# The same instructions of a fused forward and backward kernel in another order, with other PSUM banks

## The chip, the cores and the metric

The kernel runs on one core of a Trainium2 chip. The metric is the device time of one execution in microseconds (us). Before the change three runs took 435.45, 432.09 and 433.91 us, median 433.91. A core has the engines PE (matmul), DVE (vector), ACT (scalar), POOL and SP; each runs its own list of instructions strictly in order, and they meet through semaphores. In this kernel SP only issues DMAs.

## The reference

The output is `x + A(LN(x)) + B(LN(x))` and its gradients with respect to all inputs that take part, for one sequence of 2048 tokens with 512 channels, in bf16. A is a long convolution with a state space kernel, done by FFT, and B a bilinear gated MLP with 1376 hidden features:

```python
def A(q, k, v, shift_k, ssm_k, ssm_D):
    k_shift = causal_shift_conv(k, shift_k)          # 4 taps
    kv = k_shift * v
    y = irfft(rfft(pad(kv)) * rfft(pad(ssm_k)))[:S]  # per channel, L = 2 S
    return q * (y + kv * ssm_D)

def B(x, w_gate, w_up, w_down):
    return ((x @ w_gate) * (x @ w_up)) @ w_down

xn = layernorm(A_q)
out = A_q + A(xn, A_k, A_v, A_shift_k, A_ssm_k, A_ssm_D) + B(xn, B_w_gate, B_w_up, B_w_down)
# returned: out and the vjp of grad_out for the nine inputs
```

(`causal_shift_conv`, `pad` and `rfft` abbreviate the reference's own lines.)

## The kernel before

The Fourier transforms are matrix products in three steps (a first, a middle and a last DFT) with two transpositions through DRAM between them: the first writes to a DRAM tile `AX`, the middle one reads it and writes `CX`, the last one reads `CX`. The MLP runs in six strips of features; its hidden values and their gradients go to a DRAM tile `HD`.

The stages overlap, but their bulk comes in this order. The MLP strips (`mlp_rows`, `hd_store`) run beside the first DFT (`a_gen`). The weight gradients (`dw_gen`) run beside the middle DFT: `s_load(i)` reads from `AX`, `s_B` multiplies, `s_pw` is the pointwise product on DVE, `s_Bi` multiplies back, ACT copies the result out of PSUM, and four stores per step write it to `CX`. The last stage, called the F stage here, has eight steps n = 0 to 7 of two row blocks each:

- `c_load(n)` (L650) reads 1.5 MB of `CX` into one buffer `f["C"]`; for n = 0 it is split into four quarters of 384 KB, one for each quarter of `CX`'s tokens; the last quarter waits for the last four stores to `CX`, those of `s_Bi(7)`
- `last_dft(n)` (L694) does 12 matmuls on that buffer, within `c_dkv(n)` (L712); `c_load(n + 1)` can overwrite the buffer only when they are done
- `hd_load(n)` (L616) is one transposing DMA from `HD` into one of two buffers; `y_o` and `y_x` (L759, L776) multiply from it with the weights `wy`, in groups of 11 and 22 matmuls
- `c_dkv`, `c_dsk`, `dk_pair` and `c_o5` are DVE and ACT work on the convolution's gradients, with small loads and the output stores. In `c_dkv(n)` for n < 2 three small copies move rows across partitions (L712 on).

All of the 274 DMAs go through SP's one queue. SP issues them in its order; each waits for its own dependences, and also for the DMA eight places ahead of it to have landed, since eight semaphores serve the DMAs in turn. So one DMA that waits, or whose issue takes long, holds all behind it.

The order is neither that of the source nor that of a scheduler at build time. The function body records each operation as an `Op` with its engine (the call is made at L173, so every instruction in the profile carries that line). Groups of matmuls into one PSUM tile make one operation. The last line, `emit(PLAN)`, decodes a string constant at L33: 2321 numbers of two bytes, the order in which the operations are issued, and one byte for each of 408 PSUM tiles, its bank:

```python
order = struct.unpack(f"<{len(ops)}H", raw[:2 * len(ops)])
for s, b in zip(slots, raw[2 * len(ops):], strict=True):
    s.base = Q[b // 2] if s.n == 2 else halves[b]
...
    for i in order:
        for fn in ops[i].fns:
            fn()
```

Each engine's list is the part of this order that is its own: 1019 operations on PE (3174 matmuls), 654 on DVE, 371 on ACT, 274 on SP and 3 on POOL. Who waits for whom follows from the tiles and buffers that they share, in the order issued.

Of the kernel before, what the change touches and what calls it, by code (L numbers as in the profile page):

```python
# [17 lines left out]
S = 2048  # L18
D = 512
F = 1376  # L20
R = 16
# [3 lines left out]
SF = [0, 1280, 256, 512, 768, 1024]  # L25
# [4 lines left out]
RING = 28  # L30
RO = [0, 16, 24, 40, 56, 72]
EPS = 1e-5
PLAN = "c-lP|1FSC1uI&_au5H`4ZQHhO+qP}nwr$%s-*@hxyv)wFskUu4MPxt#hyu|e21J5%kRCEa2FM7RAPZ!LT#ya2LvF|ec_AM-U=UC+@DKzcAS8r>&=3Z~LO2Ky?H~f=fTR!;qC!Nd1;rp5#D=&K3(7+rC<^f)KBR>N;3Wklgk+E(DnLOf06C!$)P{;s2?|4TC;_FQG8BO-Pz|a=V`u{1p(*r$p3n?>!Dy%s?V&W(ff`T~2Ekw`3B92nG>7`o0s25c=nG?@E_8(c&;rInD;Nj!pe4+Q6>tPPL2GCL3!pO$fPpX`y1+u101e?WOocWu5hg(y=n7?F8nlI@Fdb&XZWscyU=eJD#jq5Xz$VxXTi_E+hD$IEX22d83M*j>#KjA+4A#IZh==iUD-4HiFdKHjcGw9Ca4jr{UGN!3z<$^ZA0ZK>hQyEx(!d<}1tVcK9DsfB1-`;TSO<q-J)D4(a14&aDL4(^AS5QlM3@-UVG=wC=`krL!{m4kZox&k4CmoG+<+_a9j?M{xCuYtCxpV3kOY#$ANT+j@gdxY6qpiI;RARAk03Rs!L;}cLSq<=h)*FbhQsg}0asxL%!rvVGiJf8$XE%pVP&j>*|93-z?_&1b7M8kgL$z!8Y&9r!@F<?&ca{Vh=hQMjj#qb#wOSlo8eGwjxDeyK8IE~3|~NNY=dpFCPv1n7zJx#ZES~iurAia_Baw>!zefm<={80#MQV4*Wx-{k8@!IguqC+AERLq=0}I!U^%L6LXV@cJ`TqYI09cn1MG;e;0?Tkw{QR(;%FR$8?XRQ#7Q_7$Kf;_j}ve@&cK=22@B#ZEQGVMFc!hixEZ(LHtd33u^V>B9@rCm;XGV`i?BBq#Xi^<n^8Y3hW&8>4#Yut5a;4#+>3{B3LeHII3E|{VqAhtaVt*6=va%kV{;meF>nPI#}ZhVVqt8oPbIMh)uuW4ga%SQiit;Y5DlgwG?b3xFgk_}s3p~*M%0joQxj@R?WqHu#8Oxq%V1e7hvo4EPN&m2gU;Y7Y)j{`0=A>ecm=OwREkE?DF(%)Yj_=F(G9$bx9~RJ!Mk`5@8bh}h_UGr#-X_M7@y!%e1`GpIljP`_zGX+8+?oJ@I8LOj~JigV1GJ~7jY(Cz*#h#E>bI+Lp$&je#S5O6~Ezk{DD957yiaS_!ohYh#Vy#CZU9sh!T^Mk*B#dg630ex<r?09$lfUv>S)u0BQt{={=mqeRu{g;Z({_L6n1XQZC9(A*dJa#9i2%_TYIMMR_PBC8Ok&f>Kf_3Qegf427j|l$Y{RcuGxaC@qzs{8W-kQE4heWvLuRpmda;GEjL+LP;qiWuyuei6T=)sze2-AQhs*RD_CBF)B`(s4``yEL4T6QZ>p-*{C`#q#Cq@I#M_4M2n~g^`!1}jTX~&8cAKKGxeqQG@3Th7FtVvXe_O!Z8V0q(l}a2YiK)7pdECOp3*aVPA_N@ZKO@Km-f>{+DVgX8kroTWwehD&>#9iyXhv~pqF%nR?uNuN>k_p-GlK|lUCAl`b)p)H~pkt^or2Ep;L69z`dr2befJ)825l4(Qyjv!nyG71iht`<lF~(M`!3grFH3CdY8dvbeY^OT1AiPBQ2o2beql+yE~NGWpP<uHkaL*%i%uJJ@W1gMRZ^3Gv#z~TrQW}#dYzVxcDxC3+0Bmgf5Xw?4rA2F0_l_hPudZxEtX{I(0!Vgp1;)xu`CN8|_B9Brd6o=3=>+Zn{h6lDiphyvySzx|uGoo8Tt73a+B7<i1fG`c5GvNTN_kS%wiLqC}F)u8OPbX1P!jT4uYku9{2Xs=F`}R>Db2m&#3X<J@EyULwn4m)b><t~B2*bSqpM*N<Ym{H~KL;0n4zuCOcOin?O1xGUj0yJ)h+EpiK7ESc+~N(_l3@g%w=kl3=!#g&*6Uy?{7NhpaWnWU7Gu8XVTYPwpklq>DZxU#OCOD(A+jg)s?T{qX=^>961ZI@QkNqVW{GD;>H<LbJ4u9xfW`nbNXzU$|*O9pA+a!P;K&^2-cTn=gM2D&D$sT<^yN(xCXxnzzjEK6M>$t`)LnQQL0xE5}!Yw4;<E7#hsbk(JX6q8jhi?nfVT{daw+Pl@Rjue$5QbI~fDJd?crHqu73Q}ImNkyqFm86PPm8`PHZFBcr2Ukz(N=LWWt#jL5K6jKdOHC;#1tg#3mHaZ;)t6e*KsHltx$hphhwhPk?4G!%?wNb;UbvU;m1`oe-5dATHI)zUqx<AOyD#pmYbftrGifZ1<eU5Mez?T^(<R~cZi8zsNjVuO=M<chQ*j4rFFRcq=_s9~t8|mj(p`E;FX<`0rJwYdzS2Tk%3w*&Y512*%jq~hXW$_+R7T2gx8G&ty)F}vlF@R&4U>H?GmntnZjU?U`p9s}%70vIX)A4{m4tNdWQ-hi17wg4lx#dl=E_8wB$FjO{|yW=$T@k6<Y3}lJXNO2CU@4IbLZU!w?Q_$i>@eNa+_qMjFZdmiW@Jvd7<oZ#dw0umwB>S^6(;AAWLPrtd=FRQkKaoSs`O3lG{V)0%dTz%#ztMQ)WnUKH*Nf&2rUUbJtx-zTs}VTkf_y=C())-YTVdo9vL|Zo3?DkvK9(;i#OK%kWw`>Q1@!vPMq3b&`)yisRi9jiYl6j>)k&Hpk((e8<IO=F)sh&d6ywFBfE|>~hQ9E}7?q_sCwk>kdjyJ|wlcI_Ky3d{}C50p2H7IRPi+f_zra$wj#&)%c2BmaB424#<8<#D(~=Je4P+Z0tFRLvTobAde&zm*voWS8DSOxh2=7Fc;xET#j$bL%A>aBn*e;id>!#yN&L+9Fe1POkPMOuE4M4r8MQ1+?B&|E3U$Kq#3`K(;S|gb2mQ2-T5rPl{eCY32sYe{x09-r~HsM{7(MJZ}}^~0;6YZMkRIHgL`sA?!~>i5BKE={6XH!8TU+{%L$q4zRG6_rHwcu*XMrRpYL;M4WnVT0YBh}99|!BIK9htc>p(I(I90FsrUE^*JIPi96{UiKpw>J`J;T1zx+wwyT}TXg(GStZOp3eIEs2rq#-n+e&A>tRnKupZqMhr6L;WPfx+l0zvaO^gkx(Qjjltv3wP$k`izt7J5Hi0HJK*W)S6aPXhuz?={1d}(@dIKGiVHrsTcSqU*zYULtpU={>bq(fyURkno~(G@nz1cSNJM_;#@j|XYwq*#@Bf^-{5STTW@l9{i%UsE_wA9&*8Z|kLPnf&7=8s0Wai5yqK5pQZAssbQu@a+gw<e^DrLHD|iHt<e&VSvuJ63!)3Ib7SZxrNy};lt)dmRvR2co`h{y~b*-tjw6@mKx>`>QX)!ITCAGMg(h@p~ckyl>&0}~hkK^$?fhY1F-pl*=J5S>Me1H$~WIn`Gcq$*}BYc#P@o_%EC;1ou;Awn{8|g~^%1v}SgZ<XOfuFFkHq}+Un%D4JZl=xk8-M2C{D<pnUtPy-w5_h^4ZM-tX?yLb{k4HM)Q!4{H}e1;sDreFZsCr)l{@Ku?W|q2t8UWGx<$8YH{GV&b%zetAv#od>Mp&i-L;4I)Lz<KxAAt~!Pj+|4%ZPnQb*}%y{%)kk6zOodRG_dZr!5`b&)RCCAw6X>2h76dv%|#)cv|jS8EGxsjan@#<vhAvXdX^9lfVx^^c;FvE1QtDz-+~>N-83>ouyWg|qM$(Sj_RMX>QYK_}`YJ*1QMp&r&FIz^A_F+Hv)^rTMJX*ykJ=qWv|Gj*2E)|)y<=juE?qi6M;p4SU{Q6t$S4QY`rifzzadQj)<C5>gdETt8;B9_!1Yg$WZMeVhwx0n{n!kAfD^A_9USTT!kX)Kkcws>|~^H>s#YghD%zR_fs+)`Ku%V?P_hSjjlmdzSie#>G7tftkn`j*x5S_vy@rL45Q*D_YtT3d5#VJ&Tl<+j>Z+&<`2eWraZyOpyXme?9vBdcSLt%>EcLKfQE+feIZ9qqYxvd&h}M%oMQV#6$<^|R`h)5==~t7J{BqP4MBHry&(SF2+EZIq3+F*er5*-QPZ8*HO(vJuwIs#-VeVFRtZ^|S#t-X_>Yn`{fLmrb&E_Dx^uAe(9RteUm8g;v)FTLPP9b8WM2v8{H*j@lYqWCv`UO|jXw!dBXMU1e|en4Pp!cG}L^S=(t-ZM*HT#kR{1+7jz+t8KUa(097jmf3NeZfk9w&9J_<*S!CzpESsyvk?BgU9gaTj~%l8mdNJWa+_vz?6A$ZeRjfb+6}vCm+h8)u#fi1Li;d&y}hx&_P{RL6?<rR?U6mUC-&4n+ZX$4SM8bIwr}>`ewy>--&$B7&WHCeEP{{df0+1d_RF4ILjOKc<iSVs*A0C}pUG$TFYT2T^RKPA&*Dq?tUjB+Z}-f6DF4nP`$RsmFX?|<6d%=R_kS#hPvT?yI6j(>@6{Ld(S0nR(wFwBd}?3Dm-V@PQlHG{^!a>RpWK)8<$VR8#uxVKd~Tn|SM+x*uCL@{_!K^auk5S(yuP6?<y-nzzP0b@hx%cDxbNgU`!2q#@8*m8n7)8d;A{GLzLrn#+xSL)gs<Wo`)a<BZ{lnFI=-!M>bv`1zK8GWtNZ%Cu5adx_)&heALGaRaelo2tY37!-{3d;O@6cA;s^QWzMik)^ZOQlfM4!c_?3R3Z|8ga_I`rz<2(3?eu1ClC;Ps>fgj>W`k8);-|FZ4ZN8tM>M!|KewN?v7y4;_k>BYT`yGC;pY2!sd47&x;t%-C{))fq&-!crx<BX7`-6U|-{)`mHU6fb;g|X8{(|rC=lWfKtv~FK_;voMzwM9tr~a3J=AZi){-uBAfBQfFuZJKEI__`z6aJ1r>G$~8{;q%H@A<cWx8LvI`S<>_zvxf-`+l!~;2-)!{*ez66gntmP?#VJ`rse?C*B2p@)E>BU%Uo=^%iv6pYb34H}8Xjg1-A7K2%WHpm0GyJ!zl-0~w%mLWY5%0NKz9Dm$kEZh-Af9S4>gA`UcYW>N@jf*4Q=@B_n0pl1Uh1&D!%7&u^1gSW<jF(;~l4blbh08@i?NfE)6#UQxj!+*5E6<`U-2b=(uzyKGJ2&|dv$Q-H@5f%(sLI43YhJg4#4^aagQTcaGj9q}K7L3_H0)hVj1aPImivl}ru=2m40)0O?Gz#`4m>!S{914yEg5iHB82d*Jh8!I2Kc#@{AQYUzz&G80$x-{44GqplU{?-yh|q-pfq?q~x&_=KHsfI6f+G#6I4}zIcm5xGy{0<"  # L33
KB = 1024


# [1 line left out]
def kernel(  # L38
# [142 lines left out]
    def emit(plan):  # L181
        raw = zlib.decompress(base64.b85decode(plan))
# [3 lines that stand above are left out]
        with tc.manual_schedule(engines={mybir.EngineType.PE, mybir.EngineType.DVE, mybir.EngineType.Activation, mybir.EngineType.Pool, mybir.EngineType.SP}):  # L186
# [3 lines that stand above are left out]
# [426 lines left out]
    def hd_load(n):  # L616
        a, b = hd_span(n)
        ldT(out=hdP[n % 2][:, :, 0:b - a], in_=HP[n, a:b])
# [291 lines left out]
    for n in range(NCH):  # L910
# [32 lines left out]
        else:  # L943
# [4 lines left out]
            if n + 2 < NCH:  # L948
                y_load(n + 2)
                hd_load(n + 2)  # L950
    emit(PLAN)

# [98 lines left out]
```

## Time and profile before

| what | value |
|---|---|
| median of three runs | 433.91 us (432.09 to 435.45) |
| profiled execution, span | 429.5 us |
| PE busy | 419.6 us, 98% |
| DVE busy | 352.8 us, 82% |
| ACT busy | 267.3 us, 62% |
| weight loads of PE | 204.1 us, 48% |
| DMA moved | 124.65 MB, queue of SP 91.7% of 16 engines |
| clock of PE | 1.00 throughout |
| `CX` stores, issue to landing | 4.5 us (median of 32, 384 KB each) |
| `c_load(n)`, issue to landing | 8.7 us (median of 7, 1536 KB each) |
| `hd_load(n)`, issue to landing | 12.8 us (median of 8) |
| `hd_load(n)`, length of the issue on SP | 7.73 to 11.04 us, median 9.73 |

Spans and starts are of one profiled execution; the runs' times are taken apart from it. A busy PE means that a matmul was in flight; matmuls are pipelined, and their ends are modelled, so starts are the safer reading. A row of the issue queue on SP gives the start and the length of the issue instruction, not of the transfer. "Waits" name who released an engine that was idle, as inferred from semaphores.

The stage windows of the trace (length, then busy time and instructions of PE, weight loads, DVE, ACT and POOL, then clock, share of the DMA engines and GB/s) around the start of the F stage and in it:

```profile
275.00:292.00 17.00, 14.02 (x88) 6.56 (x87) 4.32 (x6) 7.96 (x11) 0.00 (x0) 1.00 0.99 342
292.00:400.00 108.00, 108.00 (x624) 49.85 (x623) 95.24 (x197) 36.58 (x41) 0.00 (x0) 1.00 1.09 292
```

### The profile page before, as it was taken

How to read it: one execution, taken by the hardware profiler on the slowest of the kernel's cores; microseconds unless marked ns; L12 is line 12 of the kernel's file. 1: busy time of each engine (PE TensorE's matmuls, PEld its weight loads, DVE VectorE, ACT ScalarE, POOL GpSimd, SP SyncE). 2: the span in 40 equal slices, each digit the busy share in tenths (PEclk: the TensorE clock that was granted, in tenths of full speed). 3: DMA queues.
4: the chain of work that ended last, by engine and by line, in shares of the span. 5: the costliest groups of instructions: out<-in, count | busy, mean ns of one | idle time of the engine just before them, and what ended most of it. 6: DMA issues, size and time to landing. Idle time of an engine off the chain costs nothing.

```text
span 429.5 us, 8151 instructions
## 1 busy us (share of the span) xinstructions
PE 419.6 (98%) x3174; PEld 204.1 (48%) x3174; DVE 352.8 (82%) x684; ACT 267.3 (62%) x374; POOL 3.5 (1%) x9
## 2 busy tenths in 40 slices
PE   7999999999999999999999999889999999999996
PEld 4665455754454333544444344444444544444443
DVE  6799979998549989899999981044869989999996
ACT  2986879698554998988989963664244340313323
POOL 1000000000000000000000000000000000000000
PEclk9999999999999999999999999999999999999999
DMA  7997787959796979989989989999999999999933
GB/s 249 401 405 240 281 305 264 370 214 381 295 338 200 322 274 306 316 254 338 321 250 315 340 282 254 241 363 336 265 290 267 310 256 317 306 282 301 284 150 124
DMA packets 94878, 124.65 MB, mean 290 GB/s; under 512 B 53748, under 2 KB 63865, under 8 KB 93816
## 3 DMA queue, kind: packets, MB, share of 16 engines
q1 hardware_dynamic: 94840, 124.13, 91.7%
q8 instruction: 25, 0.41, 0.4%
q14 instruction: 13, 0.11, 0.1%
HBM read 57.10 MB, written 54.04 MB: 259 GB/s over the span
## 4 chain that ended last, share of the span: by engine, by line
PE 91%; DMA 6%; DVE 1%; SPq 1%; issue 1%; ACT 0%; ACTq 0%
PE PP L173 91%; DMA big<-CX 4%; DMA big<-in_goT_dram 1%; DVE big L173 1%; SPq L173 1%; ACT big L173 0%; ACTq L173 0%
## 5 line engine op out<-in xcount | busy, mean ns | idle before, releaser
L173 PE MATMUL PP<-big 128*128 128x512 bf16 (+9 forms) x3174 | 419.6, 347 | 5.8 <-issue 1.8
L173 PEld LDWEIGHTS <-big 128*128 128x128 bf16 (+5 forms) x3174 | 204.1, 98 | 221.0 <-issue 65.2
L173 DVE TENSOR_TENSOR big<-big 128x1024 bf16<-128x1024 bf16 (+4 forms) x465 | 269.3, 629 | 46.0 <-ACT big L173 42.6
L173 ACT CAST big<-PP 128x512 bf16<-128x512 f32 (+2 forms) x314 | 225.2, 780 | 90.0 <-PE PP L173 74.8
L173 ACT ACTIVATE big<-big 128x512 bf16<-128x512 f32 (+3 forms) x30 | 19.1, 645 | 40.8 <-DVE big L173 40.8
L173 DVE CAST big<-PP 128x512 bf16<-128x512 f32 (+1 forms) x37 | 32.3, 873 | 11.9 <-PE PP L173 10.0
L173 ACT COPY big<-PP 128x1024 bf16<-128x1024 bf16 x25 | 24.9, 1019 | 21.5 <-PE PP L173 21.5
L173 DVE SCALAR_TENSOR_TENSOR big<-big 128x1 f32<-128x1 f32 (+2 forms) x52 | 25.5, 498 | 0.6 <-ACT big L173 0.2
L173 DVE BATCH_NORM_STATS2 big<-big 128x6 f32<-128x512 bf16 x16 | 10.8, 679 | 2.7 <-DMA big<-in_x_dram 2.6
L173 DVE TENSOR_TENSOR big<-big,PP 128x512 bf16<-128x512 bf16 x14 | 9.5, 682 | 4.1 <-PE PP L173 4.0
L173 DVE SCALAR_TENSOR_TENSOR big<-big,PP 128x512 f32<-128x512 bf16 x14 | 9.5, 682 | 3.3 <-PE PP L173 3.3
L173 DVE TENSOR_SCALAR big<-big 128x1 f32<-128x1 f32 (+1 forms) x28 | 7.0, 259 | 0.2
L173 POOL MEMSET big<- 128x1536 bf16 (+2 forms) x3 | 2.8, 950 | 256.0 <-PE PP L173 252.7
L173 ACT ACTIVATE big<-PP 128x512 f32<-128x512 f32 x2 | 1.2, 598 | 5.5 <-PE PP L173 5.5
L173 DVE RECIPROCAL big<-big 128x2 f32<-128x2 f32 (+1 forms) x9 | 1.4, 155 | 3.7 <-ACT big L173 3.7
L173 DVE BATCH_NORM_AGGREGATE big<-big 128x2 f32<-128x6 f32 x16 | 2.8, 177 | 0.2
L173 ACT ACT_TABLE_LOAD x1 | 1.3, 1283 | 0.7 <-PEq L1039 0.7
L173 DVE DVE_READ_ACCUMULATOR big<-big 128x1 f32 x16 | 1.3, 81 | 0.0
L173 DVE DVE_READ_ACCUMULATOR big<-big,PP 128x1 f32 x14 | 1.1, 81 | 0.0
L173 DVE MEMSET big<- 128x1 f32 (+1 forms) x2 | 0.2, 112 | 0.8 <-PEq L1039 0.8
L173 DVE COPY big<-PP 128x1024 bf16<-128x1024 bf16 x1 | 0.7, 685 | 0.0
L173 ACT ACTIVATION_READ_ACCUMULATOR big<-PP 128x1 f32 x2 | 0.4, 194 | 0.0
(6 smaller groups left out, 0.9 us busy)
## 6 DMA issues: line engine op xcount, KB each, us to landing
HD<-big SPq DMA_DIRECT2D x32, 384.0 KB, 8.2
AX<-big SPq DMA_DIRECT2D x16, 768.0 KB, 5.1
big<-AX SPq DMA_DIRECT2D x16, 768.0 KB, 7.4
CX<-big SPq DMA_DIRECT2D x32, 384.0 KB, 4.5
out_dram<-big SPq DMA_DIRECT2D x44, 256.0 KB, 3.1
big<-CX SPq DMA_DIRECT2D x7, 1536.0 KB, 8.7
big<-in_v_dram SPq DMA_DIRECT2D x16, 256.0 KB, 6.2
big<-in_w_dram SPq DMA_DIRECT2D x4, 768.0 KB, 6.5
```

Source lines behind the costliest of these rows:

```text
L173: o.fns.append(lambda: f(*[fix(x) for x in a], **{kk: fix(x) for kk, x in k.items()}))
```

## The change

One line differs, the string of the plan. It is described as found by a search over drawn DMA times that counts dependent VectorE steps in full.

```diff
-PLAN = "c-lP|1FSC1uI&_au5H`4ZQHhO...
+PLAN = "c-l2rW4LZTj7`#@=ki?Jwr$(C...
```

Decoded, both plans hold the same 2321 operations, and both kernels the same 8151 instructions. At another place in their engine's list stand 832 of the 1019 operations of PE (by up to 44 places), 559 of DVE's 654 (40), 273 of ACT's 371 (126), 245 of SP's 274 (43) and 2 of POOL's 3; 235 of the 408 PSUM tiles have another bank. On SP, around the start of the F stage, the lists run so (numbers are places in SP's list; "store" is an output):

| before | after |
|---|---|
| 174 to 177: the four `CX` stores of `s_Bi(7)` | 175 to 178: the four `CX` stores of `s_Bi(7)` |
| 178: `hd_load(0)` | 179: store of a weight gradient |
| 179: `c_load(0)`, last quarter | 180: `c_load(0)`, last quarter |
| 180, 181: `y_load(0)`, `y_load(1)` | 181: `hd_load(0)` |
| 182: last part of `wy` | 182: a small copy of `c_dkv(0)` |
| 183, 184: two stores | 183: `c_load(1)` |
| 185: `c_load(1)` | 184: `y_load(0)` |
| 186: a small copy of `c_dkv(0)` | 185: store |

Further on, `hd_load(2)` stands at 204 ahead of `c_load(3)` at 206 where before `c_load(3)` (206) stood directly ahead of `hd_load(2)` (207). On PE the `s_Bi(7)` group of matmuls whose result goes to the last `CX` stores stands later, and `last_dft(0)` earlier. In the middle stages the load of the weights of strip 4 (768 KB) has moved behind the `s_load`s that it stood ahead of.

## The prediction

> **What bounds the kernel now.** I read the page's busy shares first, then the chain of waits, then the queue that the chain runs into.
>
> ```profile
> PE 419.6 (98%) x3174; PEld 204.1 (48%) x3174; DVE 352.8 (82%) x684; ACT 267.3 (62%) x374; POOL 3.5 (1%) x9
> PE PP L173 91%; DMA big<-CX 4%; DMA big<-in_goT_dram 1%; DVE big L173 1%; SPq L173 1%; ACT big L173 0%; ACTq L173 0%
> ```
>
> PE is busy for 98% of the span, and the chain that ended last is PE for 91% of it. Matmuls are pipelined, so a busy PE need not be at its peak; I took the time from one matmul's start to the next. A 128x512 follows another after 216 ns (median), a 256-column one after 109, a 128-column one after 56, with the clock at 1.00 throughout. Against these spacings the whole execution loses 11.9 us. Some 6 of them are changes of tile size (154, some 93 ns extra each, and the new order has 154 as well); the other 5.6 are seven stops. The chain in order of time shows the large late ones:
>
> ```profile
> 127.58 148.87 PE PP L173 x1408
> 276.45 1.77 issue
> 278.22 1.50 PE PP L173 x12
> 279.72 0.02 issue
> 279.74 10.12 DMA big<-CX
> 289.86 0.04 issue
> 289.90 102.24 PE PP L173 x595
> 392.14 9.06 DMA big<-CX
> 401.20 0.04 issue
> 401.24 18.34 PE PP L173 x95
> ```
>
> From 127.58 to 276.45 PE runs without a break. Then `last_dft(0)` stops for 1.93 us until the last quarter of `c_load(0)` has landed (278.13; the page calls most of it "issue"), `last_dft(1)` for 1.38 until `c_load(1)` has (289.86), `last_dft(7)` for 0.55 until `c_load(7)` has (401.20). One more stop of 0.17 stands at 127.19 (an `s_load`), and about 1.6 in the first 12 us. So a new order of the same work can win at most 0.17 + 1.93 + 1.38 + 0.55 = 4.03 us after the start, 0.9%, while a bad one can cost any amount. Why the two loads are late stands in SP's queue, start and length of each issue:
>
> ```profile
> 260.17 3.23 SPq L173 DMA_DIRECT2D CX<-big  x4
> 263.50 10.77 SPq L173 DMA_TRANSPOSE big<-HD  x1
> 274.46 0.51 SPq L173 DMA_DIRECT2D big<-CX  x1
> 275.02 1.05 SPq L173 DMA_DIRECT2D big<-in_x_dram  x2
> 276.11 0.43 SPq L173 DMA_DIRECT2D big<-in_wy_dram  x1
> 276.58 0.92 SPq L173 DMA_DIRECT2D out_dram<-big  x2
> 279.74 0.59 SPq L173 DMA_DIRECT2D big<-CX  x1
> ```
>
> SP issues strictly in order, and one transposing load (`hd_load(0)`, 10.77 us) stands ahead of the 384 KB quarter on which PE waits.
>
> **The change, part by part.** Every instruction stays; each engine's order and some PSUM banks differ. My bookkeeping adds up the spacings of the matmuls ahead of a point in the new PE order, plus 3.08 us by which before's profile runs behind that sum ahead of this stage; transfers start when SP's new order and their dependences allow, with before's durations.
>
> First, `last_dft(0)`. It is reached at 274.9, 1.4 earlier than before. The quarter load now stands ahead of `hd_load(0)`. It waits for the last four CX stores, whose `s_Bi(7)` matmuls stand 1.9 us later in PE's order: issued until about 264.1 instead of 262.3, landed 4.5 later (the stores' median) at 268.6. The quarter lands 3.67 after its issue (as before) at 272.3. The 1.93 go, with 2.6 to spare.
>
> Second, `c_load(1)`. `hd_load(0)` now starts after that quarter, at 269.1, and holds SP for 9.6 (mean of the eight) to 10.7 (its own), until 278.7 to 279.8. Behind it come one small copy (0.6) and then `c_load(1)`, which landed 10.1 after issue before, behind two x loads, a 640 KB weight load and two stores; these are no longer right ahead of it, so I take 8.0, between 7.3 (`c_load(4)`) and 10.1. It lands at 287.3 to 288.4. `last_dft(1)` is reached at 286.7, so PE stops for 0.6 to 1.7; I take 1.2. The bounds: the shortest transposition (7.7) and 7.3 give 284.7, no stop; the longest (11.0) and 10.1 give 290.8, a stop of 4.1; and if the last CX stores take 7.85, as the slowest of them did, all of it is 3.35 later, a stop of 7.5. These two stops were 3.31 and become 1.2: -2.1.
>
> A figure of the Trainium skill bears on that term, DMA: Bandwidth & Descriptors, section Latency and other measured facts, on the effective bandwidth of a DMA transpose: 261 GB/s with a non-contiguous middle dimension. The trace has it slower: 1152 x 768 values of 2 bytes, 1.77 MB, land 12.8 us after issue (median of eight), which is 138 GB/s. By the page's figure the transposition would be over in an estimated 6.8 us and the second stop would vanish too; the sum uses the trace's.
>
> Third, the other stops. At 127 one 768 KB weight load has moved behind the `s_load`: -0.17. The start keeps its stops: the same 1536 KB are ahead of the load that PE waits for at 9.5 (±0.1). In the F stage `c_load(3)` now stands behind `hd_load(2)`, and has 1.4 to spare (stop 0 to 0.7); `hd_load(1)` has 0.6 to 1.6, `hd_load(5)` 0.1 to 1.8, `hd_load(4)` and `c_load(5)` gain to 3 and more. `c_load(7)` comes out at 0.1, between -0.6 and +2.3, where it was -0.55: -0.25. For the thin ones together I put +0.3 (0 to 1.5).
>
> Fourth, DVE and ACT. PE lost nothing to either after the first 10 us of before, but the tightest evacuation of a PSUM bank had only 0.05 us to spare. In both orders the shortest distance from a copy to the matmul that reuses its bank is 0.75 us, and 20 are under 1.4. Zero; bounded by 20 hand-offs late by 0.1 each, 2.0. It is covered by the queue of matmuls between them. If that cover goes, PE waits directly. A dependent DVE step right behind its predecessor starts 0.72 us after it instead of 0.60 for 128x1024; there are 95 such neighbours before and 97 after, 0.24 us on an engine that idles 76. Zero as well. PSUM banks enter only through whom a group waits for.
>
> Fifth, the end. From the last matmul (419.57) to 429.5 both orders hold the same list, one small DVE step aside: 0 ± 0.15.
>
> The sum is -2.1 - 0.17 - 0.25 + 0.3 = -2.2: a span of 427.3. The profiled execution's 429.5 stand 4.4 under the median of the runs, so 431.7.
>
> A second rule would make the whole account different. TensorE: Matmul & The Clock Gate, section Back-to-back issue gap, puts a stream of weight loads and matmuls in a real kernel at about 131 ns for 512 columns and 81 for 128, and gives 216 and 56 for isolated ones. This trace shows 216 and 56 in the full stream, so the measurement decides. By the page's 131 the 1328 full matmuls would hold an estimated 113 us of hidden waits, and an order could win tens of us.
>
> **The rivals.** *Slower: `c_load(1)` trapped behind `hd_load(0)`.* Moving one load ahead of the long issue puts the next behind it. It decides from the start of `hd_load(0)`: beyond 270.7 instead of 269.1 the new stop reaches the old 3.31, and each us later is one of loss. For it: CX stores that landed after 5.0 and 7.85 instead of 4.5, which this quarter waits for, and the DMA queue's share of 99% in 275 to 292. With the slow end (stop 4.3 to 7.5, thin loads +0.3 to +1.5) the zone is 1 to 4.2 worse: 435 to 439. Against it: PE has 2.6 to spare at `last_dft(0)`, and the traffic ahead of `c_load(1)` is less.
>
> *All removable stops go.* A short transposition as at 363.9 (7.73), and c_loads of 7.3: -4.0, span 425.5, 429.9; with the gap of the fastest run of before (432.09 - 429.5 = 2.6) 428.1. Against it: six of eight transpositions took over 9.
>
> *Nothing changes.* The stops move to `c_load(1)`, `c_load(3)`, `hd_load(5)` and `c_load(7)`, or tight PSUM hand-offs open up: 433 to 435. For it: several slacks under 1 us, with durations that spread by 3.
>
> **How the numbers follow.** My forecast, 430.4 to 433.3, gets 0.50; the slower rival 0.20; all stops gone 0.13; nothing changes 0.17. One per cent is 4.3 us, about what a measurement of this kernel can tell from no change (its runs spread by 3.4). Faster by it means under 429.6: most of the second rival's low half and little else, 0.12. Slower means over 438.2, the slow end of the first rival (stop near 7.5) and unforeseen waits inside the unbroken stretches: 0.14. The rest is 0.74. The range leaves out about a tenth at each end: 429.2 to 436.0; the forecast's own stands above.
>
> **What would show it.** In the changed profile the gap before `last_dft(0)` is gone, the quarter's issue stands ahead of the transposition at about 268.6, `c_load(1)` is issued at 279 to 281 and lands at 287 to 289, with a stop of about 1. The matmuls' spacing stays at 216, and PE's sum of stops falls from 5.6 to some 3.5. I'd be wrong if PE shows waits on ACT or DVE beyond 10 us, if a stop over 3 stands before `last_dft(1)` or `last_dft(3)`, or if an `hd_load` that now has under 2 us ends a wait.

## The result, and the profile after

| | before | after |
|---|---|---|
| median of four runs each | 434.68 us (432.09 to 435.67) | 429.90 us (429.42 to 430.72) |
| profiled execution, span | 429.5 us | 427.5 us |
| PE idle at the start of the F stage (262 to 298) | 3.0 us | none |
| PE idle in the rest of it (298 to 425) | 0.4 us | 1.9 us |

The ratio is 0.9899, with a 95% interval of 0.9866 to 0.9931. Later, on two chips, the changed kernel came out at 0.9984 (0.9952 to 1.0015, which includes no change) and 0.9970 (0.9942 to 0.9998) of the kernel before, and the kernel before against itself at 1.0016 (0.9985 to 1.0046). Over all runs on these chips and one more, 91 of the kernel before have a median of 432.0 (middle eight tenths 429.7 to 434.3), and with those of the first measurement 26 of the changed kernel one of 430.4 (429.3 to 432.1). So the gain is nearer to 0.2 to 0.4% than to the 1.0% of the first measurement, whose four runs of the kernel before lay high (median 434.68 against 432.0; whether by the chip or by chance is open), and the spread is smaller.

The busy shares are those of before. The chain that ended last is another, as the page's fourth part shows:

```profile
PE 419.5 (98%) x3174; PEld 203.7 (48%) x3174; DVE 352.8 (83%) x684; ACT 266.5 (62%) x374; POOL 3.4 (1%) x9
...
PE PP L173 70%; DVE big L173 17%; DMA out_dram<-big 3%; DMA big<-in_K_dram 2%; DMA big<-in_x_dram 2%; DMA big<-in_goT_dram 1%; SPq L173 1%; ACT big L173 0%; DVEq L173 0%
```

The 4% of `CX` loads are gone, and 17% of DVE and 3% of output stores have come in. SP's queue around the start of the F stage, start and length of each issue:

```profile
261.67 3.33 SPq L173 DMA_DIRECT2D CX<-big  x4
265.83 0.47 SPq L173 DMA_DIRECT2D out_dram<-big  x1
269.60 0.49 SPq L173 DMA_DIRECT2D big<-CX  x1
270.18 7.31 SPq L173 DMA_TRANSPOSE big<-HD  x1
277.60 0.59 SPq L173 DMA_DIRECT2D big<-big  x1
278.28 0.59 SPq L173 DMA_DIRECT2D big<-CX  x1
```

The quarter of `c_load(0)` goes out at 269.60, ahead of the transposition, and lands at 273.35; `last_dft(0)` starts at 274.65 without a stop. The transposition holds SP for 7.31 us, where it held it for 10.77 before. `c_load(1)` goes out at 278.28 and lands at 285.05; `last_dft(1)` starts at 286.35, also without one. PE's timeline from 260 to 300 is one row with no idle time (start, length, form, count):

```profile
259.87 40.40 PE L173 MATMUL PP<-big 32*64 32x512 bf16 x263
```

All of PE's late stops now lie further on, and wait for other engines. The waits of PE from 298 to 425 (engine waited for: us in all, times, longest):

```profile
PE PP L173 <- DVE big L173: 1.3, 2, 0.9
PE PP L173 <- ACT big L173: 0.6, 1, 0.6
```

They are three: 0.61 before 331.87, 0.91 before 345.94 and 0.38 before 367.43. The timeline of the engines leads up to the first (start, length, engine, operation, and in brackets the idle time before it and who ended it):

```profile
330.08 3.63 DVE L173 TENSOR_TENSOR big<-big 128x1024 bf16<-128x1024 bf16 x5 [2.73 <-DMA out_dram<-big]
330.81 1.01 ACT L173 CAST big<-PP 128x1024 bf16<-128x1024 f32 x1 [1.52 <-DVE big L173]
...
331.87 1.46 PE L173 MATMUL PP<-big 128*128 128x512 bf16 x6 [0.61 <-ACT big L173]
```

Read backwards: PE waits for an ACT copy (`c_y(3)`) that empties its PSUM bank; that copy writes `f["y"]` and waits for a DVE step of `c_y(2)` that still reads it; that step overwrites a tile of `f["e"]` and stands 2.73 us until the output store of that tile has landed. The chain has the store: issued at 322.30, 7.76 us to landing.

```profile
321.87 0.43 DVE big L173
322.30 7.76 DMA out_dram<-big
330.06 0.02 issue
330.08 0.04 DVE big L173
```

### The profile page after: what moved, and what is told of

Read it like the earlier page. It is cut to its first block, busy times and chain, and to the rows that moved or that the text cites. A ratio compares the mean times of both kernels' runs of the same rounds, so it can differ in the third digit from the quotient of the medians.

```text
span 427.5 us, 8143 instructions
## 1 busy us (share of the span) xinstructions
PE 419.5 (98%) x3174; PEld 203.7 (48%) x3174; DVE 352.8 (83%) x684; ACT 266.5 (62%) x374; POOL 3.4 (1%) x9
## 4 chain that ended last, share of the span: by engine, by line
PE 70%; DVE 17%; DMA 8%; issue 2%; SPq 1%; ACT 0%; DVEq 0%
PE PP L173 70%; DVE big L173 17%; DMA out_dram<-big 3%; DMA big<-in_K_dram 2%; DMA big<-in_x_dram 2%; DMA big<-in_goT_dram 1%; SPq L173 1%; ACT big L173 0%; DVEq L173 0%
## 5 line engine op out<-in xcount | busy, mean ns | idle before, releaser
L173 PE MATMUL PP<-big 128*128 128x512 bf16 (+9 forms) x3174 | 419.5, 347 | 4.1 <-DVE big L173 2.3
L173 PEld LDWEIGHTS <-big 128*128 128x128 bf16 (+5 forms) x3174 | 203.7, 98 | 219.6 <-issue 66.0
L173 DVE TENSOR_TENSOR big<-big 128x1024 bf16<-128x1024 bf16 (+2 forms) x465 | 269.1, 630 | 47.0 <-ACT big L173 26.7
L173 ACT CAST big<-PP 128x512 bf16<-128x512 f32 (+2 forms) x314 | 223.9, 782 | 88.9 <-PE PP L173 47.6
L173 ACT ACTIVATE big<-big 128x512 bf16<-128x512 f32 (+3 forms) x30 | 19.1, 639 | 41.1 <-DVE big L173 40.9
L173 DVE CAST big<-PP 128x512 bf16<-128x512 f32 (+1 forms) x37 | 32.3, 876 | 12.6 <-PE PP L173 10.1
L173 ACT COPY big<-PP 128x1024 bf16<-128x1024 bf16 x25 | 25.2, 1016 | 24.0 <-PE PP L173 24.0
L173 DVE SCALAR_TENSOR_TENSOR big<-big 128x1 f32<-128x1 f32 (+2 forms) x52 | 25.1, 498 | 0.3
L173 DVE BATCH_NORM_STATS2 big<-big 128x6 f32<-128x512 bf16 x16 | 10.6, 676 | 3.0 <-DMA big<-in_x_dram 3.0
L173 DVE SCALAR_TENSOR_TENSOR big<-big,PP 128x512 f32<-128x512 bf16 x14 | 9.5, 682 | 3.8 <-PE PP L173 2.5
L173 DVE TENSOR_TENSOR big<-big,PP 128x512 bf16<-128x512 bf16 x14 | 9.5, 680 | 2.6 <-PE PP L173 2.5
L173 DVE TENSOR_SCALAR big<-big 128x1 f32<-128x1 f32 (+1 forms) x28 | 7.0, 257 | 0.3
L173 POOL MEMSET big<- 128x1536 bf16 (+2 forms) x3 | 2.8, 949 | 258.1 <-PE PP L173 258.1
L173 ACT ACTIVATE big<-PP 128x512 f32<-128x512 f32 x2 | 1.2, 597 | 2.7 <-PE PP L173 2.7
L173 DVE BATCH_NORM_AGGREGATE big<-big 128x2 f32<-128x6 f32 x16 | 2.4, 171 | 0.2
L173 DVE RECIPROCAL big<-big 128x2 f32<-128x2 f32 (+1 forms) x9 | 1.3, 149 | 0.4 <-ACT big L173 0.4
L173 DVE DVE_READ_ACCUMULATOR big<-big 128x1 f32 x16 | 1.3, 81 | 0.0
L173 DVE COPY big<-PP 128x1024 bf16<-128x1024 bf16 x1 | 0.7, 690 | 0.7 <-PE PP L173 0.7
L173 DVE DVE_READ_ACCUMULATOR big<-big,PP 128x1 f32 x14 | 1.1, 82 | 0.0
L173 DVE MEMSET big<- 128x128 bf16 (+1 forms) x2 | 0.2, 112 | 0.8 <-PEq L1039 0.8
L173 ACT ACTIVATION_READ_ACCUMULATOR big<-PP 128x1 f32 x2 | 0.4, 194 | 0.0
```

Of the source, the lines that this page charges most:

```text
L173: o.fns.append(lambda: f(*[fix(x) for x in a], **{kk: fix(x) for kk, x in k.items()}))
```

## The experiments

All but the controls edit the order after it is decoded; an entry (o, ref) puts operation o directly behind operation ref, and so shifts it within its own engine's list alone (the added line makes L173 into L174 in these profiles):

```diff
-        order = struct.unpack(f"<{len(ops)}H", raw[:2 * len(ops)])
+        order = list(struct.unpack(f"<{len(ops)}H", raw[:2 * len(ops)]))
+        for o, ref in MOVES:
+            order.remove(o)
+            order.insert(order.index(ref) + 1, o)
```

Ratios are to the kernel before on the same chip. "Idle" is PE's idle time as its timeline gives it.

### Is it the place of the transposition?

```diff
+MOVES = [(1285, 1655)]    # on the changed kernel: hd_load(0) directly ahead of the quarter
```

> The changed kernel with one move undone: hd_load(0) stands directly ahead of the last quarter of c_load(0) again. Theory (the gain at the start of the F stage is SP's order of these two): the quarter is issued only when the transposition's issue of 7.3 to 10.8 us is over, at 273.6 to 277, lands 3.7 later, and last_dft(0), reached at 274.7, stops for 2.7 to 6; last_dft(1) then has no stop of its own or a small one; the median comes back by 2.5 to 6 us, to 432 to 436. Rival (the gain is the earlier or better fitted work of PE and ACT around it, and the place of the transposition is of no weight): no stop over 0.5 at last_dft(0), median within 1 us of 429.9.

Measured: 438.57 us, ratio 1.0139 (1.0078 to 1.0201). SP's queue and PE's timeline of this kernel:

```profile
266.61 10.49 SPq L174 DMA_TRANSPOSE big<-HD  x1
277.29 0.50 SPq L174 DMA_DIRECT2D big<-CX  x1
```

```profile
281.02 19.31 PE L174 MATMUL PP<-big 128*64 128x512 bf16 x100 [5.96 <-DMA big<-CX]
```

The theory holds, at the far end of its numbers: the quarter waits for the transposition's issue, and PE idles 5.96 us before `last_dft(0)`. The transposition's length is back too, 10.49 behind the four `CX` stores and one output store that are still in flight, against 7.31 behind the quarter, by when the `CX` stores have landed (269.47). The median is 2.6 us above the expected 432 to 436; the last section has a part of that.

### Is it enough to move SP's entries?

Three versions of the kernel before, with one, then several of SP's moves.

```diff
+MOVES = [(1790, 1802)]    # the quarter ahead of hd_load(0)
```

> The kernel before with the last quarter of c_load(0) moved ahead of hd_load(0), and nothing else. Theory: the stop of 1.93 us at last_dft(0) goes, but hd_load(0), the two x loads, a weight load and two stores still stand ahead of c_load(1), which is issued at 279 to 283 and lands 7 to 10 later at 286 to 293, where PE wants it at 286.4: the second stop stays at 1.4 or grows to as much as 6. Time between -1.5 and +3 us against the kernel before. Rival (moving the quarter alone is the whole gain): both stops gone, -3 us.

Measured: 435.03 us, ratio 1.0059 (1.0024 to 1.0095). The first stop is gone, the second has grown from 1.21 to 5.2: the theory, and the second half of the rival in the prediction (a load trapped behind what is ahead of it). `c_load(1)` went out at 279.98 behind two x loads, a weight load and two stores, and landed 12.49 us later.

```diff
+MOVES = [(1790, 1802), (1793, 1815), (1794, 1793), (1284, 1794), (1246, 1284), (1680, 1246)]
+# the quarter first; c_load(1) ahead of the x loads, the weight load and both stores
```

> The kernel before with the quarter ahead of hd_load(0) and also c_load(1) directly behind hd_load(0), ahead of the two x loads, the weight load and the two stores. Theory: c_load(1) is issued when the transposition's issue is over and last_dft(0) is done, at 277.5 to 281, lands 6.8 to 8 later, and the second stop is 0 to 2.5 us: of 3.3 us of stops at the start of the F stage 1 to 3.3 go, span 426.2 to 428.5, with PE's other stops as in the kernel before (0.55 at last_dft(7), none on DVE or ACT). Rival (the other order of PE, DVE and ACT is needed for the gain): the two stops together stay above 2.5 us.

Measured: 437.03 us, ratio 1.0109 (1.004 to 1.0178). The theory fell. `c_load(1)` went out at 278.28 as in the changed kernel and PE still stopped, for something else; one line each from the timelines of ACT and PE:

```profile
291.79 0.59 ACT L174 CAST big<-PP 128x512 bf16<-128x512 f32 x1 [9.52 <-DMA out_dram<-big]
```

```profile
292.43 0.64 PE L174 MATMUL PP<-big 128*64 128x512 bf16 x2 [4.65 <-ACT big L174]
```

One of the stores now behind `c_load(1)` takes out strip 4's last weight gradient. It went out at 280.57 and landed 11.14 us later; ACT can't write the next gradient into that tile before, and with ACT's queue stuck, `last_dft(1)` has no free PSUM bank. In the kernel before the same copy starts at 284.03, right after that store's landing at 283.95: a wait that cost PE nothing was just short enough.

```diff
+MOVES = [(1790, 1802), (1793, 1815), (1794, 1793), (1284, 1794), (1680, 1284)]
+# as before, but that store between hd_load(0) and c_load(1)
```

> The kernel before with the quarter ahead of hd_load(0), then the store of strip 4's last weight gradient, then c_load(1), and the two x loads, the weight load and the other store behind that; in e3 the stores stood behind c_load(1) and the first of them, which an ACT copy waits for, landed 8 us later than before and held PE for 4.6 us. Theory (e3's second stop is that store alone, SP's order of these few entries is the whole gain): the store is issued at about 277.2 and lands by 285, c_load(1) is issued at 278.3 and lands at 285 to 287, PE's stops at the start of the F stage are 0 to 1 together instead of 3.3. Rival (PE's and ACT's other order is needed, since the copy that makes the store's data ends at 272 in the old order and at 266 in the new): ACT's wait for the store or c_load(1) still hold PE for more than 2 us.

Measured: 433.58 us, ratio 1.0037 (1.0007 to 1.0067). Neither `last_dft(0)` nor `last_dft(1)` stops, as the theory had it, but PE idles 2.23 us for ACT before 296.31: an ACT copy of `c_o5(1)` waits 3.75 us for the store of `c_o5(0)` to land, which the moved entries have pushed back. Two late `hd_load`s cost 0.71 and 0.24 more, before 312.24 and 396.37. Of the theory's gain nothing is left in the time. By its own number (over 2 us of ACT's waits) the rival holds, though by another store than the one it named.

```diff
+MOVES = [(1246, 1793)]    # on the changed kernel: strip 4's store behind c_load(1) again
```

> The changed kernel with one more of its moves undone: the store of strip 4's last weight gradient stands behind c_load(1) again instead of ahead of the quarter. Theory (this move of a store, which the prediction did not cost, is a needed part of the gain): the store is issued at 279 to 280 and lands 8 to 11 later at 287 to 291, ACT's copy waits for it, and last_dft(1), reached at 286.3, stops for 1 to 5 us: 1 to 6 us more than the changed kernel. Rival (the store's place is of no weight in the new ACT order): no change beyond 0.5.

Measured: 436.76 us, ratio 1.0104 (1.0044 to 1.0164). PE waits 3.3 us for ACT before `last_dft(1)`, as expected; the median stands 6.3 above that of the changed kernel on this chip (e7 below), a little more than the expected 1 to 6. In the changed kernel that store goes out at 265.83, since the ACT copy that makes its data ends at 265.8; in the old order it ends at 272.2. So the gain at the start of the F stage needs two things at once: the quarter ahead of the transposition (e1) and this store out of the way of `c_load(1)` (e8). That it also needs ACT's and PE's new order, which has the store's data ready by then, is argued and not shown: e5, in the old order, lost both stops too, and paid for another store.

### Where do the new stops in the F stage come from?

```diff
+MOVES = [(1879, 1878)]    # on the changed kernel: the store of e up to the step for block 1
```

> The changed kernel with one store of 256 KB (the gradient rows of y_x for block 1) moved five places up SP's list, to directly behind the DVE step that makes its data. In the changed kernel it is issued 6.8 us after its data is ready, lands at 330.06, and DVE stands 2.73 us for it before a step of c_y(2) that overwrites its tile. Theory A (three stops of PE, 0.61 at 331.3, 0.91 at 345.0 and 0.38 at 367.1, all come from DVE's lateness after that wait): DVE's wait goes, all three stops go, span 425.3 to 426, median about 1.9 under 429.9. Theory B (only the first stop comes from it, the later two from DVE's own order): the stop at 331 goes, those at 345 and 367 stay, -0.6. Theory C (the store is late in landing wherever it stands, since the queue is full): nothing changes.

Measured: 431.64 us, ratio 0.9988 (0.9959 to 1.0016). None of the three theories can be read from it: the tile also holds block 0, whose last addition comes later on DVE, so that here block 0's rows of the gradient go out without it, and that addition waits 5.2 us for the store to land. What it does show is the price of such a wait: PE idles 2.4 us for DVE in two places behind it (0.90 before 327.40 and 1.54 before 330.75), and then has no stop at 345 or 367.

```diff
+MOVES = [(1920, 1892)]    # on the changed kernel: c_load(3) directly ahead of hd_load(2)
```

> The changed kernel with c_load(3) ahead of hd_load(2), as in the kernel before. In the changed kernel c_load(3) is issued at 314.9 behind that transposition; SP's entry eight places behind it, a store, waits till 321.6 for its landing, and the store behind that (the one that DVE waits for at 327.4 to 330.1) is issued at 322.3. Theory A: c_load(3) is issued at 307, the two stores go out at about 320, DVE's wait of 2.73 us shrinks to under 0.7, and the three late stops of PE (0.61, 0.91, 0.38) go with it: 1.3 to 1.9 us less than the changed kernel on the same chip. Theory B: only the first goes, -0.6. Theory C (later landings of hd_load(2) or hd_load(3) take its place): no gain.

Measured: 431.58 us, ratio 1.0007 (0.9974 to 1.004). Theory C. `c_load(3)` goes out at 307.94, but with its 1.5 MB in flight the transposition behind it takes longer:

```profile
307.94 0.62 SPq L174 DMA_DIRECT2D big<-CX  x1
308.65 10.70 SPq L174 DMA_TRANSPOSE big<-HD  x1
```

That is 10.70 us instead of 7.21, and the store that DVE waits for goes out at 324.17, no earlier than in the changed kernel. DVE waits 2.59.

```diff
+MOVES = [(1851, 1895), (1879, 1851)]    # block 0's last addition earlier, the store behind it
```

> The changed kernel with one DVE step of 0.42 us (the last addition of y_x for block 0) three places up DVE's list, into a gap in which DVE idles, and the store of its tile behind it, four places up SP's list. (In e4 the store stood ahead of that addition, so that block 0's rows went out without it, and the addition then waited for the store.) The store that DVE waits for at 327 to 330 is issued at 318 instead of 322.3 to 324 and lands by 326. Theory (DVE's wait of 1.0 to 2.7 us there makes the two stops of PE at 331 and 345, when it is long: 2.73 gave 0.61 and 0.91, 2.59 gave 0.5 and 0.97, 0.98 gave none; the stop of 0.4 to 0.7 at 367 is DVE's own order): DVE's wait under 0.3, no stop at 331 and 345, the one at 367 stays; 0 to 1.5 us less than the changed kernel on this chip. Rival (DVE is behind there anyway): stops at 331 or 345 remain at 0.3 or more.

Measured: 430.85 us, ratio 0.9996 (0.9967 to 1.0024). The store goes out at 319.07, the wait before that step is gone and so is the stop at 331; but the next step on DVE (`dk_pair`, whose tile another store is taking out) waits in its place, and the stop at 345 stays, at 0.99. PE also idles 1.39 for ACT before 301.82, ahead of all that was moved. The line of DVE:

```profile
330.99 3.03 DVE L174 TENSOR_TENSOR big<-big 128x1024 bf16<-128x1024 bf16 x4 [2.05 <-DMA out_dram<-big]
```

```diff
+MOVES = [(1851, 1895), (1879, 1851), (2059, 2058), (2002, 2059), (2105, 2104), (2083, 2105), (2085, 2083)]
+# f1, and the DVE steps that free the PSUM banks for 345 and 367 ahead of two others each
```

> f1, and two more places on DVE: the step that empties the PSUM bank for the matmuls at 345 goes ahead of two steps that nobody waits for, and the one for the matmuls at 367 ahead of two steps of dk_pair. Theory: all three late stops are gone whatever DVE's lateness, the medians stand 0.5 to 2 us under the changed kernel on this chip. Rival: DVE is so full there (82% of the span) that the steps put back are late next, and a stop of 0.3 or more shows elsewhere between 320 and 400.

Measured: 431.08 us, ratio 0.9979 (0.9952 to 1.0005). The rival: the stops at 345 and 367 are gone, and 0.57 before 360.04, 1.00 before 367.46 and 0.31 before 388.49 stand there instead, all for DVE; 0.45 before 303.19, for ACT, is ahead of all that was moved. No version tried beats the changed kernel.

### The two kernels again

> The changed kernel itself once more, on the chip of the other experiments. If its three late stops (331, 345, 367) belong to its order, they are there again, each between 0.3 and 1.5 us, and the start of the F stage has no stop over 0.5; span 427 to 429. If they were an accident of one execution, they lie elsewhere.

Measured: 430.46 us, ratio 0.9984 (0.9952 to 1.0015). Half of each: the stops at 331 and 345 are not there, PE idles twice near 367 (0.84 and 0.50), and at the start of the F stage there is one, from `c_load(1)`, on PE's timeline:

```profile
288.54 3.75 PE L173 MATMUL PP<-big 128*64 128x512 bf16 x22 [1.75 <-DMA big<-CX]
```

> The changed kernel again, as the control for f1 and f2 on their chip. Theory (its order leaves less to the transfers): its runs lie between 429 and 432 but for single ones, its median 0.5 to 3 us under that of the kernel before on the same chip; the stop at 367 is there again with 0.3 to 0.8, a stop at last_dft(1) of 0 to 2. Rival (the first measurement's 1.0% was the chip and few runs): within 0.3%.

Measured: 430.63 us (428.86 to 433.18, 12 runs), ratio 0.9970 (0.9942 to 0.9998), which is the rival's 0.3%; the median is also 1.1 us under that of the kernel before, within the theory's 0.5 to 3, so the two are not told apart. There is no stop at the start of the F stage, and near 367 there is more than the expected 0.3 to 0.8. PE idles 0.70 before 302.15 for ACT, and 0.85 before 346.42, 1.20 before 366.77 and 0.51 before 369.31 for DVE. Two of these stand behind a wait of ACT or DVE for a transfer, one line each from the timelines:

```profile
300.18 1.01 ACT L173 CAST big<-PP 128x1024 bf16<-128x1024 f32 x1 [4.39 <-DMA out_dram<-big]
302.15 2.03 PE L173 MATMUL PP<-big 128*32 128x512 bf16 x20 [0.70 <-ACT big L173]
364.16 0.69 DVE L173 TENSOR_TENSOR big<-big 128x1024 bf16<-128x1024 bf16 x1 [1.45 <-DMA big<-in_x_dram]
366.77 2.03 PE L173 MATMUL PP<-big 128*64 128x512 bf16 x20 [1.20 <-DVE big L173]
```

> The kernel before itself, for a second profile of it. Theory (it loses time at the same two places in every execution, by amounts that its transfers draw): stops at last_dft(0) and last_dft(1), together between 1.5 and 6 us, the transposition behind the four CX stores holds SP for 10 to 11 us. Rival (the 3.3 us of the first profile were an accident): together under 1 us, other stops elsewhere.

Measured: 432.15 us (428.94 to 434.96, 12 runs). One of the two stops is there: PE idles 2.17 before `last_dft(0)`, behind this queue, and none before `last_dft(1)`.

```profile
261.99 3.25 SPq L173 DMA_DIRECT2D CX<-big  x4
265.34 11.11 SPq L173 DMA_TRANSPOSE big<-HD  x1
276.64 0.51 SPq L173 DMA_DIRECT2D big<-CX  x1
```

Over the executions with the changed kernel's F stage (e4 and f2 follow below the table), DVE's wait for a store near 330 goes with PE's two stops behind it:

| kernel | DVE's wait | PE idle at 331 | at 345 |
|---|---|---|---|
| e1 (all some 9 us later) | 2.77 | 0.65 | 0.89 |
| changed kernel | 2.73 | 0.61 | 0.91 |
| e6 | 2.59 | 0.48 | 0.94 |
| f1 (wait one step later) | 2.05 | 0 | 0.99 |
| f3, changed kernel | 1.60 | 0 | 0.85 |
| e8 (all some 4 us later) | 1.23 | 0 | 0.23 |
| e7, changed kernel | 0.98 | 0 | 0 |

The stop at 345 comes with a wait of more than 1 us, the one at 331 with one of more than 2 at that very step. That f2 lost the stop at 345 by DVE's order alone, with a wait of 1.95, agrees: it is DVE's lateness that PE meets there. e4, with a wait of 5.2 us that ends 4 us earlier, met it in two other stops and had none at 345.

Two more waits go with a stop in the same way: ACT's for an output store near 299, and DVE's for a load of x near 364.

| kernel | ACT's wait near 299 | PE idle at 302 | DVE's wait near 364 | PE idle at 366 |
|---|---|---|---|---|
| f1 | 5.07 | 1.39 | 0 | 0 |
| e4 | 4.42 | 0.75 | 0 | 0 |
| f3, changed kernel | 4.39 | 0.70 | 1.45 | 1.20 |
| f2 | 4.13 | 0.45 | 1.13 | 1.00 |
| e1 (all some 9 us later) | 3.55 | 0 | 0.38 | 0.24 |
| changed kernel | 3.49 | 0 | 0 | 0 |
| e7, changed kernel | 3.26 | 0 | 1.14 | 0.84 |
| e6 | 3.19 | 0 | 0.68 | 0.47 |
| e8 (all some 4 us later) | 2.37 | 0 | 0.53 | 0.40 |

The stop at 302 is ACT's wait less 3.7 us in all four executions that have it, and the one at 366 is 0.13 to 0.30 short of DVE's wait for the load. So that stop goes with a load that lands late, and not with DVE's own order alone, as the expectation for f1 had it for the idling near 367. Another stop of 0.35 to 0.51, some 2.5 us behind that place, stands in seven of the nine, with or without that wait; its cause is open.

## Why the prediction was right, point by point

The time lies in the range, and the span of 427.5 is 0.2 from the forecast 427.3. Two terms were off in opposite directions, and a third between span and time, so it is in part luck that the span comes out this close.

**`last_dft(0)`: right.** The order of events is the one predicted; the quarter landed at 273.35 (272.3 forecast), with 1.3 to spare instead of 2.6. e1 shows that this place is what does it: with the transposition back ahead, 5.96 us of idling.

**`c_load(1)`: mechanism right, size off.** The step that gave a stop of 1.2 took 9.6 to 10.7 us for the issue of `hd_load(0)` and 8.0 for the landing; they were 7.31 and 6.76, both under the lower ends that I used (7.7 and 7.3). The durations were taken from rows in which much was in flight ahead of the transposition. With the `CX` stores landed, `hd_load(0)` took 7.2 to 8.2 in eleven executions; directly behind them 10.5 to 11.1 in three. In e7 the stop was 1.75; in the first profile, in f3, and in e4, e6, f1 and f2, which have the same order up to there, there was none. The forecast of 1.2 is thus between 0 and 1.75, and the gain at these two stops was 3.0 us in the profiles (0.9 more than forecast) and 1.2 if e7 is set against the first profile.

**What the part on `c_load(1)` left out.** It counted the two stores as traffic that is no longer ahead, and did not ask who waits for them to land. e3, e5 and e8 show that one wrongly placed store costs 2.2 to 4.65 us there through ACT. In the changed kernel that was arranged; I was right without having looked.

**The other loads: right in sum.** The stop at 127 is gone in every execution of the changed order (in those of the old one it was 0.17 to 2.1, and absent in e2), `last_dft(7)` no longer stops, and no `hd_load` or `c_load(3)` ended a wait of PE in any execution of the changed F stage. In some executions a load of `K` ends a wait at 84 instead, of up to 0.9.

**DVE and ACT: wrong.** "Zero; bounded by 20 hand-offs late by 0.1 each, 2.0" is the step that failed, by the prediction's own sign (waits of PE on ACT or DVE beyond 10 us). PE idled for them behind 298 for 1.9, 1.3 and 3.3 us in the three executions of the changed kernel, and not at all in the two of the kernel before. I looked at the distance between a copy and the matmul that reuses its bank, with DVE's durations as in before, but not at what DVE and ACT themselves wait for. In the two profiles of the kernel before, DVE waits for no output store in the F stage; in the changed order a store of a tile that DVE overwrites lands late near 330, DVE stands for up to 2.77 us, and at 83% busy it is late for the next 15 us. ACT's wait for a store near 299 and DVE's for a load of x near 364 are the same kind of term; they make 0.70 and 1.20 of the 3.3 in f3. These waits are read from the traces, and their link to PE's stops is shown by the two tables above. Why the store near 330 is late is only argued: `c_load(3)`, eight places ahead of the store before it, is behind `hd_load(2)`. It was not isolated, since e6, which undid that swap, lengthened the transposition instead.

**The end: right.** From the last matmul's start to the end of the span 4.4 us before, 4.2 after. That matmul starts at 425.16 before; the 419.57 of the prediction is where the chain that ended last leaves PE.

**The sum.** -2.2 forecast, -2.0 in the two profiles: -3.0 instead of -2.1 at the start of the F stage, and +1.5 (1.9 for DVE and ACT, less the 0.4 of `last_dft(7)`) instead of about zero behind it; the rest is 0.3 less idle time in the first 15 us (2.3 before, 2.0 after), the 0.17 at 127 and 0.1 at the end. One reading that no term uses was wrong: 154 changes of tile size at 93 ns would be 14 us and not some 6. In the trace the 93 ns hold for about half of them, those away from 128x128 tiles, some 7 us.

**From span to time: wrong.** "429.5 stand 4.4 under the median of the runs" took the difference for something that lies around the span. In each of the runs that list both, time less span is 1.73 to 1.92. The rest of the 4.4 is that this one execution of the kernel before was shorter than the median one; fewer stops are the likely reason, not shown. With 1.8 the forecast would have been 429.1, nearer to the measured 429.90 than 431.7 is.

**The rivals.** The slower one has its mechanism confirmed (e2: 5.2 us at `last_dft(1)`), but not its place: the traffic that traps the load is what the change moved away. "All removable stops go" came true at the places it named in the first profile, and lost 1.9 of it to stops that it didn't know. "Nothing changes" described the two later chips well: the stops move, and 0.16% and 0.30% remain.

## What to carry to other kernels

A store's landing is a dependence like any other: before an order is changed, list for each moved DMA who overwrites its source, on ACT and DVE too, and follow the wait from there to the bound engine. One profile is one draw of the transfers; where PE has 1 to 4 us of stops in 430, take the span and time of several runs, and subtract spans from spans. In a kernel with PE at 98%, DVE at 83% and the queue at 91%, a stop that is taken away at one place shows at another, and single moves of an order that was made as a whole (e2, e3, e5, f1, f2) brought nothing.

## What I had not expected of the hardware

The length of the issue of a transposing load on SP goes with what is in flight ahead of it: 6.7 to 7.2 us for `hd_load(2)` in eight executions without a large load directly ahead, 10.0 to 11.8 in six behind `c_load(3)`; the same instruction, the same bytes.

A stop can cost more than its length. In e1, after 5.96 us of idling, the windows (length, busy time and instructions of PE, weight loads, DVE, ACT and POOL, then the granted clock) read:

```profile
276.00:278.00 2.00, 0.00 (x0) 0.00 (x0) 0.00 (x0) 0.00 (x0) 0.00 (x0) 1.00 1.28 290
...
280.00:281.00 1.00, 0.00 (x0) 0.01 (x1) 0.00 (x0) 0.00 (x0) 0.00 (x0) 0.50 0.04 12
...
284.00:285.00 1.00, 1.00 (x4) 0.32 (x3) 1.00 (x1) 0.05 (x1) 0.00 (x0) 0.50 0.00 0
285.00:287.00 2.00, 2.00 (x9) 0.86 (x8) 2.00 (x4) 0.00 (x0) 0.00 (x0) 0.77 0.86 240
```

The clock falls to 0.50 at 279.1, within the stop, and comes back at 285.9, some 5 us after work resumes (281.02); from 284 until then 128x512 matmuls follow each other at 426 ns instead of 216, so that these 5 us do the work of some 2.5, and the stop costs an estimated 8.4 in all. The same came with idling of 3.3 (e8), 4.65 (e3) and 5.2 us (e2), and once with 2.17 (f4, from 281.6 on; here and in e8 the clock falls only after the stop has ended), while with 1.75 (e7), 1.77 (the first profile) and 2.23 (e5) the windows stay at 1.00. The Trainium skill, TensorE: Matmul & The Clock Gate, section HAM oscillation, gives idle gaps of more than about 3.4 us as what brings the clock down; the three longest stops here agree, e8 and f4 show that a shorter one can be enough. It bears on the two kernels: 20 of the 91 runs of the kernel before had a mean clock under 0.9975, and these had a median of 433.4 against 431.6 for the others; of the 26 of the changed kernel one had. Shorter stops at the start of the F stage would make this rarer, which no term of the prediction had; that they are the cause is argued from the traces above, not shown.
